# ELU chain spread over two steps for the first block only, and the attention steps, loads and weight steps around it re-timed

## The chip, the cores and the metric

The kernel runs on one core of a Trainium2 chip. The metric is the device time of one execution in microseconds (us), the median of several runs. Five queues of instructions run beside each other and wait for one another through semaphores: PE (matmuls, with their weight loads), DVE (vector work), ACT (activations, copies and casts), POOL (hardly used here) and SP, which issues nearly all DMAs. Each works through its own instructions in program order.

## What is computed

```python
# attention: chunks of 32 queries, keys from 16 before to 8 after the chunk, plus 8 memory keys
scores = scale * np.matmul(q_c, k_full.transpose(0, 1, 3, 2))
a = np.exp(scores - np.max(scores, axis=-1, keepdims=True))
a = a / (np.sum(a, axis=-1, keepdims=True) + 1e-09)
out[:, :, c_start:c_end] = np.matmul(a, v_full)
# x: (4 * 768, 8 * 64) = (3072, 512)
h = x @ w_in                                             # (3072, 2048)
g = np.where(h > 0.0, h, np.exp(np.minimum(h, 0.0)) - 1.0)
x = g @ w_out                                            # (3072, 512)
return ((x @ w1) * (x @ w2)) @ w3 @ w_out2               # (3072, 512)
```

## The kernel before

Every wide product is made of three matmuls (`mm3`, lines 124 to 126): each operand is kept as a rounded high part and the remainder, its low part, and high*high, high*low and low*high are summed in PSUM. So every operand that PE reads has to be split first: ACT writes the high part, DVE subtracts it from the value and writes the low part.

**The first two products.** The 3072 tokens are cut into 8 blocks of 384, and `w_in`, `w_out` into 16 slices each. The main loop counts n = 0 to 129, n = 16 * block + slice. In pass n PE works out `mm_h(n)`, 12 matmuls of 384 columns, one slice of h, into one of two PSUM banks (`bank4`, `bank5` in turn). ELU of that slice goes through five steps: `elu_exp` (two ACTIVATEs on ACT, lines 474 and 475), `elu_max` (DVE, line 480, the last reader of the bank), `elu_hi` (ACT, line 484) and `elu_lo` (DVE, line 488). Two passes later `mm_x(n - 2)`, again 12 matmuls, adds the slice's share to the block's result in four other banks. So `mm_h(n + 2)` needs `elu_max(n)`, and `mm_x(n)` needs `elu_lo(n)`. In the kernel before, `elu_exp(n)` and `elu_max(n)` stand in pass n, `elu_hi(n)` and `elu_lo(n)` in pass n + 1.

**Block borders.** In the first two passes of a block `mm_x(n - 2)` goes ahead of `mm_h(n)`, and after the second one `store_x1` copies the four finished banks to four tiles (ACT, DVE, ACT, DVE: lines 115 and 117) and stores them to DRAM (line 501). These tiles come from a pool of four, `f`, which the weight jobs use as well.

**Attention.** Tokens are worked on in 24 groups G of 128, three to a block. A group is a chain: `at_turn`, `at_turn2` (PE transposes, ACT copies: lines 289 to 306), `load_next` (q and k of group G + 1), `at_scores` (PE, 317), `at_max` (DVE 334, 335 and an ACT exponential, 336), `at_sum` (DVE 342 to 345), `at_norm` (DVE 354), `at_flip` (DVE 365), `at_values` (PE, 376), `at_out` (split into `xhl`, 120 and 121), `load_next_v`. Groups 0 to 2 come ahead of the loop, interleaved by hand in the string `START` (a letter for a step, a digit for the group, `f` for one step of the weight feed). The others are put into numbered slots, two to a pass: slot 2n runs in the middle of pass n and slot 2n + 1 after `mm_x(n - 2)` (in the first two passes of a block slot 2n comes after `mm_x` and slot 2n + 1 after `mm_h`). `base(G)` is the slot in which a group's chain begins; its steps follow at 0, 1, 1, 2, 3, 4, 5, 6, 8, 8 and 9.

**Weights.** `w_in` and `w_out` come as doubles and are rebuilt as float32 in 32 jobs of the feed. One `feed.step()` does a cast on ACT (172) and one Prelu (159), and on DVE a shift (163), an or (167) and a subtraction (175), spread over three jobs in a row. Five steps stand in `START`, and two in each pass of the first block until they are used up. Weights of the later products go through like jobs in the slots (`rebase`, `mid_low`, `mid_split`) of the groups from 6 on, and every `mid_low` starts a next load of 512 KB.

Of the kernel before, what the change touches and what calls it, by code (L numbers as in the profile page):

```python
# [19 lines left out]
def tile_kernel(  # L20
# [40 lines left out]
    GPB = TB // GQ  # L61
    FF1 = w_in.shape[1] // P
# [3 lines left out]

    LATER = (10, 11, 12, 13, 14, 15, 25, 26, 27, 28, 29, 30, 31)

    START = "t0 u0 f s0 t1 f m0 u1 s1 z0 n0 m1 p0 t2 v0 u2 s2 f z1 n1 p1 o0 m2 v1 f z2 n2 p2 o1 v2 f o2"
    SCALE = 1.0 / float(D) ** 0.5  # L70
    assert GQ == P and KEYS == 64 and KT == 4 and HP == 4 and DM == 512

# [177 lines left out]
    def load_qk(G):  # L250
        if G >= NG:
            return
        b, g = divmod(G, GPS)
        t0 = g * GQ - LEFT
        p0, n1 = max(0, -t0), min(LEFT + RIGHT, S - t0 - P)
        kn_g = k_t[G] = at_tile(G, qk_p, [P, 2, H, D], "kn") if 0 < G < GPB else kn
        q_t[G] = at_tile(G, qk_p, [GQ, H, D], "qn")
        eng = nc.scalar if G == 0 else nc.sync
        eng.dma_start(out=q_t[G], in_=by_token(q, b, g * GQ, (g + 1) * GQ))
        nc.sync.dma_start(out=kn_g[p0:P, 0], in_=by_token(k, b, t0 + p0, t0 + P))  # L260
        nc.sync.dma_start(out=kn_g[0:n1, 1], in_=by_token(k, b, t0 + P, t0 + P + n1))
        if g == 0 or G < GPB:
            nc.sync.dma_start(out=kn_g[LEFT + RIGHT:CH, 1], in_=by_token(mem_k, b, 0, NM))

    def load_v(G):
        if G >= NG:
            return
        b, g = divmod(G, GPS)
        t0 = g * GQ - LEFT
        p0 = max(0, -t0)  # L270
        vw_g = v_t[G] = at_tile(G, v_p, [P, 2, H, D], "vw") if 0 < G < GPB else vw
        nc.sync.dma_start(out=vw_g[p0:P, 0], in_=by_token(v, b, t0 + p0, t0 + P))
        for c in range(NCG):
            t1 = t0 + (c + 1) * CH
            n1 = min(LEFT + RIGHT, S - t1)
            nc.sync.dma_start(out=vw_g[c * CH:c * CH + n1, 1], in_=by_token(v, b, t1, t1 + n1))
            if g == 0 or G < GPB:
                nc.sync.dma_start(out=vw_g[c * CH + LEFT + RIGHT:(c + 1) * CH, 1], in_=by_token(mem_v, b, 0, NM))
# [147 lines left out]
        slots.setdefault(int(at), []).append((at, len(slots.get(int(at), ())), fn, arg))  # L426

    def base(G):
        return 2 * FF1 * (G - GPB) // GPB, "slow"

    GM = 2 * GPB
    others = [Job((raw_rows, w_out2, c, 0), store=wod[c]) for c in range(FF2)]
# [3 lines left out]
    for G in range(GPB, NG):  # L436
        s0, pace = base(G)
# [16 lines left out]
    def at_step():  # L454
        store_next()
        for _, _, fn, arg in sorted(slots.pop(slot_at[0], ()), key=lambda x: x[:2]):
            fn(arg)
        slot_at[0] += 1
# [19 lines left out]
    def elu_max(n):  # L478
        e = eg_t[n]
        nc.vector.scalar_tensor_tensor(out=e, in0=e, scalar=-1.0, in1=h_t.pop(n), op0=ALU.add, op1=ALU.max)  # L480
# [5 lines left out]
    def elu_lo(n):  # L486
        g = g_t[n]
        nc.vector.tensor_tensor(out=g[:, 1, :], in0=eg_t.pop(n), in1=g[:, 0, :].bitcast(F32), op=ALU.subtract)  # L488
# [82 lines left out]
    with tc.manual_schedule():  # L571
        def weight(i):
            if i < FF1:
                return Job((raw_cols, w_in, i), slot=i)
            return Job((raw_rows, w_out, i - FF1, 0), slot=i)

        jobs, due = [], {}
        order = sorted(range(2 * FF1), key=lambda i: i if i < FF1 else i - FF1 + 2)
        for i in order:
            due[i] = len(jobs)  # L580
            jobs.append(weight(i))
        first_late = min(due[i] for i in LATER)
        feed = Feed(jobs)

        load_qk(0)
        make_identity(nc, ident)
        nc.gpsimd.memset(kn[0:LEFT, 0], 0.0)
        nc.gpsimd.memset(vw[0:LEFT, 0], 0.0)
        for c in range(NCG):
            for s in range(2):  # L590
                nc.gpsimd.memset(odd[c * CH:(c + 1) * CH, s], float(c % 2 == s))
        feed.load(1)
        load_qk(1)
        feed.load(2)
        load_v(0)
        load_qk(2)
        load_v(1)
        feed.load(3)
        load_v(2)
        feed.load(5)  # L600
        one = dict(t=at_turn, u=at_turn2, s=at_scores, m=at_max, z=at_sum, n=at_norm, p=at_flip, v=at_values, o=at_out)
        for what in START.split():
            if what == "f":
                feed.step()
            else:
                one[what[0]](int(what[1]))
        load_qk(GPB)
        load_v(GPB)
        early_psum.close()
        psum_x = ctx.enter_context(tc.tile_pool(name="psum_x", bufs=1, space=PSUM))  # L610
        for i in range(KT):
            PS[i] = psum_x.tile([P, 512], F32, name=f"bank{i}")
        NH = NB * FF1
        for n in range(NH + 2):
            j, f, at, last = seq[n] if n < NH else (NB, n - NH, n - NH, False)
            first = at < 2 and n >= 2
            if j == NB - 1 and f == 0:
                store_next()
                mid_ctx.close()
                at_ctx.close()  # L620
                late = ctx.enter_context(tc.tile_pool(name="late", bufs=1, side="right"))
                ab_jobs = [(c, r) for c in range(FF2) for r in range(2)]
            if n == FF1:
                feed.until(len(feed.jobs) - 1)
                raw_ctx.close()
                mid_ctx = ExitStack()
                pools["raw"] = mid_ctx.enter_context(tc.tile_pool(name="raw2", bufs=2, side="right"))
                pools["st"] = mid_ctx.enter_context(tc.tile_pool(name="st_p", bufs=2, side="right"))
                mid_load(2)

            def x():
                if n >= 2:
                    if n < FF1 + 2:
                        feed.until(due[FF1 + seq[n - 2][1]])
                    mm_x(n - 2)
                    if at == 1 and n < NH:
                        store_x1(j - 1)
                if n < FF1:
                    feed.step()
                at_step()  # L640

            if first:
                x()
            if n < NH:
                if j == 0:
                    feed.until(due[f])
                mm_h(n)
            if 1 <= n <= NH:
                elu_hi(n - 1)
            if n < FF1:  # L650
                feed.step()
            if 1 <= n <= NH:
                elu_lo(n - 1)
            at_step()
            if n < NH:
                elu_exp(n)
            if not first:
                x()
            if n < NH:
                elu_max(n)  # L660
            if n >= NH - FF1:

                free = [f] if n < NH else []
                if n >= NH - FF1 + 2:
                    free.append(FF1 + n - 2 - (NH - FF1))
                for slot in free:
                    if len(s_wo) < FF2 and len(s_wo) <= len(s_w3):
                        fill(slot, wod[len(s_wo)])
                        s_wo.append(slot)
                    elif len(s_w3) < 2 * FF2:  # L670
                        half, c = divmod(len(s_w3), FF2)
                        fill(slot, w3d[half][c])
                        s_w3[half, c] = slot
                    else:
                        c, r = ab_jobs.pop(0)
                        fill(slot, wabd[c][r])
                        s_ab[c, r] = slot
            if j == NB - 1:
                if f == 4:
                    load_x1(0)  # L680
                if f == 8:
                    split_x1(0)
                    load_x1(1)
        store_x1(NB - 1)
        for half in range(2):
            for c in range(FF2):
                for i in range(KT):
                    mm_wc(half, c, i)
                    if c == FF2 - 1:
                        keep_wc(half, i)  # L690
            for i in range(KT, FF2):
                c, r = ab_jobs.pop(0)
                fill(s_w3[half, i], wabd[c][r])
                s_ab[c, r] = s_w3[half, i]
        NA = NB * FF2
        for n in range(NA + 1):
            j, f = divmod(n, FF2)
            if n < NA:
                mm_ab(n)
                if f == 2 and j + 1 < NB:  # L700
                    split_x1(j + 1)
                    if j + 2 < NB:
                        load_x1(j + 2)
            if n >= 1:
                mm_o(n - 1)
                if f == 0:
                    store_out(j - 1)
# [30 lines left out]
```

## Time and profile before

| | |
|---|---|
| median of 3 runs | 1154.38 us (1153.18 to 1154.81) |
| profiled execution | 1155.27 us, its span 1153.3 us |
| before the first `mm_h` | 0 to 39.3 us |
| block 0 (passes 0 to 15) | 39.3 to about 133 us |
| blocks 1 to 7 | about 133 to 703 us |
| the last two products | about 703 us to the end |
| PE, DVE, ACT busy share | 95%, 43%, 37% |

The page gives busy shares over the whole span, so the stages have to be looked at one by one: stretches (windows) for how full each engine is, the timeline of an engine for the start of each instruction and what ended the idle time ahead of it, the table of waits for how often the same wait comes back, and the chain of waits for what ended last.

### The profile page before, as it was taken

Reading aid. Unit: us, or ns where it says so; the run is one execution under the profiler, and the core shown is the slowest. Engines: PE = TensorE matmul, PEld = TensorE weight load, DVE = VectorE, ACT = ScalarE, POOL = GpSimd, SP = SyncE. Lnnn points to the kernel's source line nnn. Section 1 sums busy time; section 2 is a strip of 40 time slices with the busy share of each in tenths; the row PEclk is TensorE's granted clock in tenths of the full one; section 3 lists DMA queues with packets and bytes.
Section 4 is the critical chain, followed back from the end, with each engine's and each line's share of the span. In section 5 each row is a group of like instructions: output and inputs, shape, how many; then the busy total and the mean of one; then the engine's idle time right before and its main releaser. Section 6 shows DMA issues by size and latency. Waiting matters only on the chain.

```text
span 1153.3 us, 20889 instructions
## 1 busy us (share of the span) xinstructions
PE 1096.8 (95%) x8800; PEld 1029.9 (89%) x8800; DVE 493.8 (43%) x912; ACT 431.1 (37%) x897; POOL 2.1 (0%) x16
## 2 busy tenths in 40 slices
PE   4688999999999999899999999999999999999998
PEld 3588889989989899899899998799999999999997
DVE  4699655565565465555555331121222212222121
ACT  3477544454454444445444341121221212222111
POOL 0000000000000000000000000000000000000000
PEclk8699999999999999999999999999999999999999
DMA  8957344543633543544531785310000101000000
GB/s 171 288 143 205 99 150 120 158 135 109 175 110 110 173 128 109 157 129 128 155 105 40 251 286 178 109 45 28 28 28 28 55 1 56 28 28 28 1 28 28
DMA packets 153100, 124.78 MB, mean 108 GB/s; under 512 B 103856, under 2 KB 136624, under 8 KB 153008
## 3 DMA queue, kind: packets, MB, share of 16 engines
q1 hardware_dynamic: 151968, 123.20, 36.3%
q8 instruction: 69, 1.13, 0.4%
q10 hardware_dynamic: 1040, 0.26, 0.1%
q14 instruction: 23, 0.19, 0.1%
HBM read 89.88 MB, written 33.55 MB: 107 GB/s over the span
## 4 chain that ended last, share of the span: by engine, by line
PE 81%; DVE 8%; ACT 5%; DMA 3%; issue 2%; SPq 0%; DVEq 0%; ACTq 0%
PE bank L124 21%; PE bank L125 20%; PE bank L126 20%; PE banks L124 4%; PE banks L126 4%; PE banks L125 4%; DMA x1d<-st 2%; PE banks L376 2%; DVE w L175 1%; DVE g L488 1%; DVE eg L480 1%; PE banks L317 1%; DVE e L354 1%; ACT w L172 1%; PE banks L291 1%
## 5 line engine op out<-in xcount | busy, mean ns | idle before, releaser
L124 PE MATMUL bank<-xhl,w 128*128 128x384 f32 x768 | 266.4, 347 | 17.5 <-DVE eg L480 16.8
L126 PE MATMUL bank<-xhl,w 128*128 128x384 f32 x768 | 259.3, 338 | 0.0
L125 PE MATMUL bank<-xhl,w 128*128 128x384 f32 x768 | 259.2, 338 | 0.0
L124 PE MATMUL bank<-g,w 128*128 128x384 f32 x512 | 176.0, 344 | 0.0
L125 PE MATMUL bank<-g,w 128*128 128x384 f32 x512 | 172.5, 337 | 1.7 <-DVE g L488 0.8
L126 PE MATMUL bank<-g,w 128*128 128x384 f32 x512 | 171.5, 335 | 0.0
L124 PEld LDWEIGHTS bank<-xhl,w 128*128 128x128 f32 x768 | 145.6, 190 | 27.5 <-DVE eg L480 21.6
L552 DVE TENSOR_TENSOR eg<-eg,banks 128x384 f32<-128x384 f32 x64 | 35.5, 554 | 271.7 <-PE banks L126 271.7
L125 PEld LDWEIGHTS bank<-xhl,w 128*128 128x128 f32 x768 | 145.7, 190 | 3.2 <-DVE xhl L121 0.4
L126 PEld LDWEIGHTS bank<-xhl,w 128*128 128x128 f32 x768 | 145.4, 189 | 0.0
L488 DVE TENSOR_TENSOR g<-eg,g 128x384 fp32r<-128x384 f32 x128 | 71.3, 557 | 108.2 <-ACT g L484 108.2
L484 ACT CAST g<-eg 128x384 fp32r<-128x384 f32 x128 | 65.7, 513 | 127.0 <-DVE eg L480 127.0
L125 PEld LDWEIGHTS bank<-g,w 128*128 128x128 f32 x512 | 96.2, 188 | 4.8 <-DVE g L488 4.7
L124 PEld LDWEIGHTS bank<-g,w 128*128 128x128 f32 x512 | 96.1, 188 | 2.2
L126 PEld LDWEIGHTS bank<-g,w 128*128 128x128 f32 x512 | 96.1, 188 | 0.0
L551 ACT COPY eg<-bank 128x384 f32<-128x384 f32 x64 | 30.7, 480 | 170.4 <-PE bank L126 170.4
L480 DVE SCALAR_TENSOR_TENSOR eg<-eg,bank 128x384 f32<-128x384 f32 x128 | 69.9, 546 | 56.0 <-ACT eg L475 55.7
L120 ACT CAST g<-eg 128x384 fp32r<-128x384 f32 x64 | 32.8, 512 | 141.4 <-DVE eg L552 141.4
L124 PE MATMUL banks<-xhl,w 128*128 128x384 f32 x256 | 85.5, 334 | 0.0
L125 PE MATMUL banks<-xhl,w 128*128 128x384 f32 x256 | 85.5, 334 | 0.0
L126 PE MATMUL banks<-xhl,w 128*128 128x384 f32 x256 | 85.5, 334 | 0.0
L474 ACT ACTIVATE eg<-bank 128x384 f32<-128x384 f32 x128 | 62.8, 490 | 48.4 <-PE bank L126 47.8
(101 smaller groups left out, 1404.9 us busy)
## 6 DMA issues: line engine op xcount, KB each, us to landing
raw<-in_moe_w_dram SPq DMA_DIRECT2D x32, 512.0 KB
raw<-in_moe_w_out_dram SPq DMA_DIRECT2D x20, 512.0 KB
w3d<-st SPq DMA_DIRECT2D x16, 512.0 KB
wabd<-st SPq DMA_DIRECT2D x16, 512.0 KB
w<-w3d SPq DMA_DIRECT2D x16, 512.0 KB
w<-wabd SPq DMA_DIRECT2D x16, 512.0 KB
raw<-in_moe_w_in_dram SPq DMA_DIRECT2D x12, 512.0 KB
x1d<-st SPq DMA_DIRECT2D x32, 192.0 KB
```

The source lines that it names most:

```text
L120: nc.scalar.copy(hi, src)
L124: mm(o, lhsT=w_hi, rhs=x_hi, start=start, stop=False)
L125: mm(o, lhsT=w_hi, rhs=x_lo, start=False, stop=False)
L126: mm(o, lhsT=w_lo, rhs=x_hi, start=False, stop=stop)
L172: nc.scalar.copy(job.to[:, 0, :], job.f if src is None else src)
L376: mm(o, lhsT=vw[cc, u, 2 * hp + r, :], rhs=pT[cc, r, hp, u, :], start=u == 0, stop=u == 1)
L474: nc.scalar.activation(e, h_t[n], AF.Relu, scale=-1.0)
L480: nc.vector.scalar_tensor_tensor(out=e, in0=e, scalar=-1.0, in1=h_t.pop(n), op0=ALU.add, op1=ALU.max)
L484: nc.scalar.copy(g_t[n][:, 0, :], eg_t[n])
L488: nc.vector.tensor_tensor(out=g[:, 1, :], in0=eg_t.pop(n), in1=g[:, 0, :].bitcast(F32), op=ALU.subtract)
L551: nc.scalar.copy(e, pab[0])
L552: nc.vector.tensor_tensor(out=e, in0=e, in1=pab[1], op=ALU.mult)
```

## The change

Four edits. In `START` the third step of the feed moves from ahead of group 1's sum to behind group 1's values, the fourth and fifth move back too, group 2's maximum (the third group) comes ahead of group 0's output, and the loads of group 3 (the fourth group; `k` and `w`) stand right behind that output and no longer behind the whole string. `base` grows by one slot, for groups 3 to 23. And from pass 16 on all five ELU steps of a slice stand in the pass that made it: `elu_exp` ahead of the slot's work, `elu_hi` and `elu_lo` right behind `elu_max`. For passes 0 to 15 the order is the old one.

```diff
-    START = "t0 u0 f s0 t1 f m0 u1 s1 z0 n0 m1 p0 t2 v0 u2 s2 f z1 n1 p1 o0 m2 v1 f z2 n2 p2 o1 v2 f o2"
+    START = "t0 u0 f s0 t1 f m0 u1 s1 z0 n0 m1 p0 t2 v0 u2 s2 z1 n1 p1 m2 o0 k3 w3 v1 z2 n2 p2 f o1 v2 f o2 f"
...
     def base(G):
-        return 2 * FF1 * (G - GPB) // GPB, "slow"
+        return 2 * FF1 * (G - GPB) // GPB + 1, "slow"
...
-        one = dict(t=at_turn, ..., o=at_out)
+        one = dict(t=at_turn, ..., o=at_out, k=load_qk, w=load_v)
         for what in START.split():
...
-        load_qk(GPB)
-        load_v(GPB)
...
                 mm_h(n)
-            if 1 <= n <= NH:
+            spread = n < FF1
+            if 1 <= n <= FF1:
                 elu_hi(n - 1)
-            if n < FF1:
+            if spread:
                 feed.step()
-            if 1 <= n <= NH:
+            if 1 <= n <= FF1:
                 elu_lo(n - 1)
+            if n < NH and not spread:
+                elu_exp(n)
             at_step()
-            if n < NH:
+            if spread:
                 elu_exp(n)
             if not first:
                 x()
             if n < NH:
                 elu_max(n)
+            if n < NH and not spread:
+                elu_hi(n)
+                elu_lo(n)
```

DVE ahead of the main loop, from the transpose of group 0 (`pT_376`) on, before and then after; `e_372` is group 1's exponentials, `pair1_101` group 2's scores, `w0_75` the first weight slice:

```order
L365 STREAM_TRANSPOSE pT_376<-e2_368 128x1024
L163 TENSOR_SCALAR f_315<-f_315 128x512
L167 SCALAR_TENSOR_TENSOR f_315<-raw_197,f_315 128x512
L175 TENSOR_TENSOR w0_75<-f_259,w0_75 128x512
L342 TENSOR_REDUCE sm_469<-e_372 128x8
L343 TENSOR_SCALAR sm_469<-sm_469 128x8
L344 RECIPROCAL sm_469<-sm_469 128x8
L345 TENSOR_TENSOR rc_470<-sm_469,odd_167 128x16
L354 TENSOR_TENSOR e2_475<-e_372,rc_470 128x16x32 x2
L365 STREAM_TRANSPOSE pT_478<-e2_475 128x1024
L121 TENSOR_TENSOR xhl0_73<-banks_94,xhl0_73 128x2x4x64
L334 TENSOR_REDUCE mx_482<-pair1_101 128x8
```

```order
L365 STREAM_TRANSPOSE pT_376<-e2_368 128x1024
L342 TENSOR_REDUCE sm_461<-e_372 128x8
L343 TENSOR_SCALAR sm_461<-sm_461 128x8
L344 RECIPROCAL sm_461<-sm_461 128x8
L345 TENSOR_TENSOR rc_462<-sm_461,odd_167 128x16
L354 TENSOR_TENSOR e2_467<-e_372,rc_462 128x16x32 x2
L365 STREAM_TRANSPOSE pT_470<-e2_467 128x1024
L334 TENSOR_REDUCE mx_472<-pair1_101 128x8
L335 TENSOR_TENSOR e_473<-pair1_101,mx_472 128x512
L121 TENSOR_TENSOR xhl0_73<-banks_94,xhl0_73 128x2x4x64
```

The three weight instructions are gone from between group 0's transpose and group 1's sum, and group 2's maximum and subtraction stand ahead of group 0's low part (L121).

SP at the end of `START`, before and then after; `more_`, `raw_` are weight loads, `qn`, `kn_166`, `vw_165` group 3's q, k and v:

```order
L140 DMA raw_317<-in_moe_w_in_dram 128x4x256
L148 DMA raw_467<-in_moe_w_out_dram 128x1024
L140 DMA raw_525<-in_moe_w_in_dram 128x4x256
L148 DMA raw_578<-in_moe_w_out_dram 128x1024
L259 DMA qn_582<-in_q_dram 128x8x64
L260 DMA kn_166<-in_k_dram 128x8x64
L261 DMA kn_166<-in_k_dram 24x8x64
L272 DMA vw_165<-in_v_dram 128x8x64
L276 DMA vw_165<-in_v_dram 24x8x64 x4
```

```order
L140 DMA raw_317<-in_moe_w_in_dram 128x4x256
L259 DMA qn_479<-in_q_dram 128x8x64
L260 DMA kn_166<-in_k_dram 128x8x64
L261 DMA kn_166<-in_k_dram 24x8x64
L272 DMA vw_165<-in_v_dram 128x8x64
L276 DMA vw_165<-in_v_dram 24x8x64 x4
L148 DMA raw_537<-in_moe_w_out_dram 128x1024
L140 DMA raw_579<-in_moe_w_in_dram 128x4x256
L148 DMA raw_589<-in_moe_w_out_dram 128x1024
```

Group 3's loads pass three weight loads.

DVE at the border of blocks 1 and 2, from the two copies of `store_x1` (`bank1`, `bank3`) on, before and then after; `eg` and `g` with `bank4`, `bank5` are the ELU tiles, `st` with `f` is the low part of a later weight:

```order
L163 TENSOR_SCALAR f_1665<-f_1665 128x512
L167 SCALAR_TENSOR_TENSOR f_1665<-raw_1636,f_1665 128x512
L480 SCALAR_TENSOR_TENSOR eg_1696<-eg_1696,bank4_95 128x384
L117 COPY st_1715<-bank1_596 128x384
L117 COPY st_1721<-bank3_598 128x384
L326 MEMSET banks_94 32x2x4x16
L175 TENSOR_TENSOR st_1757<-f_1665,st_1757 128x512
L488 TENSOR_TENSOR g_1772<-eg_1696,g_1772 128x384
L334 TENSOR_REDUCE mx_1776<-banks_94 128x8
L335 TENSOR_TENSOR e_1777<-banks_94,mx_1776 128x512
L480 SCALAR_TENSOR_TENSOR eg_1781<-eg_1781,bank5_96 128x384
L488 TENSOR_TENSOR g_1797<-eg_1781,g_1797 128x384
```

```order
L480 SCALAR_TENSOR_TENSOR eg_1667<-eg_1667,bank4_95 128x384
L488 TENSOR_TENSOR g_1686<-eg_1667,g_1686 128x384
L117 COPY st_1704<-bank1_596 128x384
L117 COPY st_1710<-bank3_598 128x384
L163 TENSOR_SCALAR f_1683<-f_1683 128x512
L167 SCALAR_TENSOR_TENSOR f_1683<-raw_1636,f_1683 128x512
L326 MEMSET banks_94 32x2x4x16
L175 TENSOR_TENSOR st_1775<-f_1683,st_1775 128x512
L480 SCALAR_TENSOR_TENSOR eg_1739<-eg_1739,bank5_96 128x384
L488 TENSOR_TENSOR g_1779<-eg_1739,g_1779 128x384
L334 TENSOR_REDUCE mx_1798<-banks_94 128x8
L335 TENSOR_TENSOR e_1799<-banks_94,mx_1798 128x512
```

The weight job's shift and or (L163, L167) move behind the two copies, the low part of the block's first slice (first L488) ahead of them, and the next slice's maximum and low part (second L480 and L488) ahead of the group's maximum (L334, L335).

## Rows read from the trace of the kernel before

**Rows 1.** The page, busy us (share of the span) xinstructions of each engine

```profile
PE 1096.8 (95%) x8800; PEld 1029.9 (89%) x8800; DVE 493.8 (43%) x912; ACT 431.1 (37%) x897; POOL 2.1 (0%) x16
```

**Rows 2.** Stretches: from:to, length, busy of each engine, granted PE clock, DMA share, GB/s

```profile
30.00:40.00 10.00, 3.80 (x97) 3.02 (x89) 8.83 (x17) 4.68 (x9) 0.00 (x0) 0.50 1.00 350
40.00:50.00 10.00, 6.29 (x24) 5.26 (x25) 2.62 (x5) 2.66 (x7) 0.00 (x0) 0.67 1.13 257
39.30:130.00 90.70, 76.53 (x757) 71.07 (x757) 76.58 (x143) 58.13 (x120) 0.00 (x0) 0.93 0.64 169
```

**Rows 3.** Timeline of DVE ahead of the loop: start, us, instruction [idle before <-releaser]

```profile
19.79 1.23 DVE L365 STREAM_TRANSPOSE pT<-e 128x1024 f32<-128x1024 f32 x1
24.06 0.69 DVE L175 TENSOR_TENSOR w<-f,w 128x512 fp32r<-128x512 f32 x1 [2.00 <-ACT w L172]
24.67 0.68 DVE L342 TENSOR_REDUCE sm<-e 128x8 f32<-128x512 f32 x1
27.36 1.25 DVE L365 STREAM_TRANSPOSE pT<-e 128x1024 f32<-128x1024 f32 x1
...
35.10 1.25 DVE L365 STREAM_TRANSPOSE pT<-e 128x1024 f32<-128x1024 f32 x1
...
39.28 0.69 DVE L121 TENSOR_TENSOR xhl<-pair,xhl 128x512 fp32r<-128x512 f32 x1 [0.70 <-ACT xhl L120]
```

**Rows 4.** Timeline of SP and DVE around the start of block 0

```profile
27.73 0.36 SPq L148 DMA_DIRECT2D raw<-in_moe_w_out_dram  x1
38.46 0.39 SPq L259 DMA_DIRECT2D qn<-in_q_dram  x1
...
50.51 0.69 DVE L175 TENSOR_TENSOR w<-f,w 128x512 fp32r<-128x512 f32 x1 [7.82 <-ACT w L172]
53.38 0.55 DVE L488 TENSOR_TENSOR g<-eg,g 128x384 fp32r<-128x384 f32 x1
```

**Rows 5.** Chain of waits, two of its DMAs: start, us to landing, what

```profile
38.95 7.50 DMA kn<-in_k_dram
...
225.93 4.16 DMA x1d<-st
```

**Rows 6.** Who waited for whom, whole span: us in total, times, longest

```profile
DVE st L117 <- DMA x1d<-st: 23.1, 6, 4.4
PE bank L124 <- DVE eg L480: 16.8, 15, 1.8
```

**Rows 7.** Timeline of PE at the second block border, first matmul of each piece

```profile
223.83 0.45 PE L124 MATMUL bank<-g,w 128*128 128x384 f32 x1
226.54 0.86 PE L317 MATMUL banks<-kT,qT 64*32 64x64 f32 x64
231.60 0.34 PE L124 MATMUL bank<-g,w 128*128 128x384 f32 x1
235.46 0.44 PE L124 MATMUL bank<-xhl,w 128*128 128x384 f32 x1 [1.36 <-DVE eg L480]
237.68 0.33 PE L124 MATMUL bank<-g,w 128*128 128x384 f32 x1
240.71 0.44 PE L124 MATMUL bank<-xhl,w 128*128 128x384 f32 x1 [0.79 <-DVE eg L480]
```

**Rows 8.** Timeline of SP and DVE at the same border

```profile
225.49 0.35 SPq L148 DMA_DIRECT2D raw<-in_moe_w_out_dram  x1
230.21 0.56 DVE L117 COPY st<-bank 128x384 f32<-128x384 f32 x1 [3.85 <-DMA x1d<-st]
234.85 0.56 DVE L480 SCALAR_TENSOR_TENSOR eg<-eg,bank 128x384 f32<-128x384 f32 x1 [1.69 <-ACT eg L475]
239.04 0.42 DVE L163 TENSOR_SCALAR f<-f 128x512 int32<-128x512 int32 x1
239.50 0.69 DVE L167 SCALAR_TENSOR_TENSOR f<-raw,f 128x512 int32<-128x512 int32 x1
```

**Rows 9.** Stretch in which the border's fourth store moves, columns as in rows 2

```profile
231.40:232.00 0.60, 0.60 (x5) 0.33 (x4) 0.60 (x2) 0.00 (x0) 0.00 (x0) 1.00 0.64 230
```

More of the change, by code (lines that the diff above doesn't have):

```diff
@@ L600, in tile_kernel @@
         feed.load(5)
-        one = dict(t=at_turn, u=at_turn2, s=at_scores, m=at_max, z=at_sum, n=at_norm, p=at_flip, v=at_values, o=at_out)
+        one = dict(t=at_turn, u=at_turn2, s=at_scores, m=at_max, z=at_sum, n=at_norm, p=at_flip, v=at_values, o=at_out, k=load_qk, w=load_v)
         for what in START.split():
```

## The prediction, made before the changed kernel ran

> **What bounds the kernel now.** I read the page first: PE is busy for 95% of the span, DVE and ACT for well under half [rows 1]. That says that in most of the program only PE's own instructions count, so an edit to DVE, ACT or SP can pay only where PE stands still. I therefore went through PE's timeline piece by piece, a piece being the 12 matmuls of one `mm_h` or `mm_x`. Undisturbed, a piece takes 2.08 us (for instance 235.46 to 237.68 is one, with 0.1 us more because attention work stood before it) [rows 7]. The reader is to see in that timeline which pieces are longer. Inside blocks 1 to 7 hardly any is. There are two places where PE loses time.
>
> The first is everything up to the end of block 0. The stretch 39.3 to 130 has DVE busy for 76.6 of 90.7 us [rows 2], and the largest hole in DVE is one wait of 7.82 us for a cast on ACT [rows 4]. Without it DVE is busy for 76.6 of 83 us: two weight steps a pass, ELU and attention are nearly more than DVE can do in the 4.2 us that PE needs for a pass. Block 0 is bound by DVE, and what DVE gains at its start, the block's end gains.
>
> The second is each block border that has attention in it. `mm_x` of the old block's last slice takes 2.71 us (223.83 to 226.54) where 2.19 would do; the first `mm_x` of the new block is followed by `mm_h` 3.86 us later (231.60 to 235.46), and the next one 3.03 us later (237.68 to 240.71), where 2.08 would do [rows 7]. That is 0.5 + 1.8 + 0.95 = 3.25 us a border. The table of waits says what PE waited for in the last two, `elu_max`, the reader of its bank (16.8 us in all), and it shows the cause behind it: DVE's second copy in `store_x1` waits for a store to land, 6 times, 23.1 us in all [rows 6]. Six borders, so some 19.5 us.
>
> **The start (START string).** Removed from ahead of group 1's sum: a weight step on DVE, whose subtraction waited 2.00 us for ACT. Group 0's transpose is at 19.79 and takes 1.23, so the sum can start at 21.0 instead of 24.67 [rows 3]. From sum to transpose is 2.69 us (24.67 to 27.36) [rows 3], so group 1's transpose moves to 23.7. Then come group 2's maximum and subtraction and group 0's low part on DVE, about 0.7 each as the rows of that size have it [rows 3], and two ACT operations of about 0.6 in between: group 2's sum at 28.2, its transpose at 30.9 instead of 35.10 [rows 3]. The weight steps are not gone, they now stand behind it: two steps of 0.42 + 0.69 + 0.69 [rows 4, 8], the low part of group 1 and that of group 2 follow the 1.25 us transpose. So group 2's low part, which the second matmul of `mm_h(0)` needs, starts at about 36.2 instead of 39.28 [rows 3]: 3 us earlier. The fifth weight step now comes behind it, 1.8 us more work on DVE inside block 0, which the reckoning at the next step includes.
>
> **Group 3's loads.** Before, they were issued at 38.46, behind a weight load that waited for DVE, and k landed at 38.95 + 7.50 = 46.45 [rows 4, 5]. Now only six weight loads of 512 KB stand ahead, the first issued at 27.73 [rows 4]. At 350 GB/s [rows 2] they take 9.0 us and are through at about 37.7; 512 KB of q and k at 257 GB/s [rows 2] take 2.0 us more. That gives 39.7 as the earliest; I add some 2 us because the 16 engines do not finish together, and take 42, with 46.5 (nothing gained) as the other end. Three weight loads come later by these 0.8 MB, about 3 us; the DMA share in block 0 is 0.64 [rows 2], so they have slack.
>
> What follows: before, from k's landing to the first `elu_lo` (53.38) it was 6.9 us [rows 4, 5], because `elu_exp(0)`, a weight cast and subtraction and `elu_max(0)` all stood behind group 3's transposes and copies on ACT. With the chain one slot later they stand ahead and are done while k is on its way. Left behind the landing are the transposes and copies (2.6 us), `elu_hi`, a cast, a subtraction: about 4.5 us. So the first `elu_lo` comes at 42 + 4.5 = 46.5 instead of 53.38. I take **6.5 us** for the start as a whole, and as its ends 2.4 (landing at 46.5) and 8. From there the same instructions remain for DVE, so block 0 ends earlier by as much. PE's clock was granted at 0.50 and 0.67 in these stretches [rows 2], that is at 1.2 GHz for part of them; since DVE sets the pace I count nothing for it.
>
> **Base one slot later, ELU in one pass: the borders.** Three things change at a border. (a) `elu_hi` and `elu_lo` of the old block's last slice no longer stand behind group copies on ACT, so the 0.5 us go. (b) The weight job's `mid_low`, which starts a 512 KB load, now comes behind `store_x1`. Before, that load was issued 0.44 us ahead of the stores (225.49) [rows 8], and the first store took 4.16 us [rows 5]. The fourth store, with nothing ahead of it, is copied from 230.21 to 230.77 [rows 8] and has moved 138 of its 192 KB (128 x 384 float32) by 232.0 [rows 9]: about 1.6 us. I take 1.6 for the first store too, the row of the same transfer, with 4.16 as the other end. (c) On DVE, from the waiting copy to the end of `elu_max` it was 5.2 us (230.21 to 235.41) [rows 8], with a low part, the group's maximum and subtraction and an exponential in it; now there are a shift and an or (0.42, 0.69) [rows 8], one cast and one subtraction of about 0.65, and `elu_max`: 3.4 us.
>
> Against this, ACT has the three group copies, a Prelu and `elu_hi` ahead of the first copy, so that the store is issued some 1.3 us later, seen from the next `mm_x`. Set out from that `mm_x`'s start: before, the copy waited until -1.4 and `elu_max` ended at +3.8, 1.8 us too late for +2.08. Now the copy ends its wait at -1.4 + 1.3 - 2.5 = -2.6 and `elu_max` ends at +0.8: no wait. The step after it (the 0.95) has the group's sum ahead of `elu_max` as before, with under 1 us of room by the same reckoning; I leave 0.35 us a border for it. So 2.9 us a border, **17.4 us** for six. With a landing of 4.16 again, `elu_max` ends at +3.3 and the later wait stays too: 1.1 us a border, 6.6 in all. The upper end is 3.25, 19.5 in all.
>
> The Trainium skill, page "DMA: Bandwidth & Descriptors", section "Anatomy of one DMA", puts a DMA at about 2.0 us fixed plus its bytes at 436 GB/s, fitted there on another issue path: 2.45 us for 192 KB, an estimate from that page. The 1.6 us of the fourth store is shorter than that. By that page of the skill the copy would wait 0.85 us longer, the later step would lose about 0.6 us a border, and the sum would be 3.6 us smaller, near 1134.
>
> The same page of the Trainium skill, section "Queues, rings and completion order", says that descriptors on one engine are consumed in ring order. The 4.16 against 1.6 us agrees; for group 3's early loads it speaks against the change, since the weights behind them wait.
>
> **Inside the blocks** the edit costs nothing by my reckoning. The five ELU steps are 0.5 to 0.56 each [rows 4, 8], 1.6 us from the end of `mm_h(n)` to that of `elu_max(n)`, and `mm_h(n + 2)` starts three pieces later, 6.24 us: 4.6 us are left for slot work on DVE and ACT. What hides it is that distance; the rivals price its loss.
>
> **Sum.** 1155.27 for the profiled execution, less 6.5, less 17.4, is 1131.4. The median of the runs is 0.9 below that execution: **1130.5 us**.
>
> **Rivals.** (1) *The stores still land late*, because store, v loads and weight traffic from the last slots are still in the engines. For it: the DMA share of 0.64 in block 0 shows how much is moved at times [rows 2]. Against it: the next load now stands behind. 6.5 + 6.6 gained: about 1141.5. (2) *The start gives little*: six weight loads ahead and the ragged end of the 16 engines [rows 2] let k land no earlier, or the weight steps moved out of the start's holes come back on DVE, which is nearly full. 1.5 + 17.4: about 1135.5. (3) *Slower: ACT and DVE wait for each other in each pass.* `elu_hi(n)` now waits on ACT for `elu_max(n)`, which stands behind the slot's DVE work, and `elu_exp(n + 1)` queues behind `elu_hi(n)`. In the slot with `at_values` and `at_out`, `elu_max` waits for a piece of PE (2.08), the values (about 1.2), a cast and a subtraction (about 1.3): 4.6 us, just the room that there is. From there on PE stops. If the 18 groups of blocks 1 to 6 lose 2 us each, the size of the waits of that kind now (1.8) [rows 6], that is 36 us: 1131 + 36 = 1167. Against it: in that slot the values themselves also push `mm_h(n + 2)` back by their own length. (4) *The waits only change their name*: PE stops later in the border for the next `elu_max`, and the start is given back by DVE: about 1154.
>
> **Chances.** Forecast 0.60, (1) 0.12, (2) 0.16, (3) 0.07, (4) 0.05. The forecast's own range is 1125 to 1135. Cases (1) and (2) have the same sign, so the range reaches over both, to 1143, and down to 1121, which takes both upper ends and something for waits inside block 0 that I did not count. About 0.2% is what a measurement of this kernel can tell from no change. Faster 0.88, within it 0.05, slower 0.07.
>
> **What would show it.** In the profile of the changed kernel: the first `elu_lo` near 46.5 and k's landing near 42; block 0 over some 6 us earlier; no wait of DVE's copy for a store above 2 us; the waits of `mm_h` for `elu_max` down from 15 to the few of block 0; the distance between borders about 80 us instead of 83. It would be wrong if the granted clock or the last two products changed, or if ACT's `elu_hi` were followed by PE waits inside the blocks.

## The result and the profile after

| | before | after |
|---|---|---|
| median of the runs, us | 1154.6 | 1127.88 |
| lowest to highest, us | 1153.18 to 1155.08 | 1127.37 to 1129.28 |
| ratio after / before | | 0.9773, interval 0.9756 to 0.9789 |
| span of the profiled execution, us | 1153.3 | 1127.3 |
| `elu_max(13)` starts (end of block 0) | 127.98 | 122.58 |
| from there to `elu_max(125)` (blocks 1 to 7) | 561.81 | 541.24 |

The kernel became 2.3% faster: 26.7 us between the medians, 26.0 us between the two spans. The last two rows of the table say where: 5.4 us before `elu_max(13)`, 20.6 us between it and `elu_max(125)`, and nothing in the two last products. These two distances, read from the starts of `elu_max` on DVE, are what every experiment below is measured by.

The page after, first row of busy times (answers to [rows 1]), and stretches of the kernel after (columns as in [rows 2]: length, busy of PE, PEld, DVE, ACT, POOL, granted clock, DMA share, GB/s):

```profile
PE 1092.1 (97%) x8800; PEld 1029.9 (91%) x8800; DVE 493.7 (44%) x912; ACT 430.2 (38%) x897; POOL 2.1 (0%) x16
...
30.00:40.00 10.00, 5.90 (x74) 5.31 (x75) 9.83 (x17) 4.17 (x7) 0.00 (x0) 1.00 1.06 334
40.00:50.00 10.00, 8.74 (x99) 7.40 (x99) 6.41 (x13) 7.37 (x16) 0.00 (x0) 1.00 0.87 258
...
127.80:677.00 549.20, 549.12 (x5311) 529.24 (x5309) 297.94 (x553) 267.50 (x566) 0.00 (x0) 1.00 0.52 152
```

The same stretch of blocks 1 to 7 in the kernel before:

```profile
133.06:703.06 570.00, 555.21 (x5309) 529.77 (x5309) 297.45 (x552) 268.48 (x565) 0.00 (x0) 1.00 0.49 146
```

The same 5309 or so matmuls: before, PE stood still for 14.8 us and was 6.1 us longer at its work; after, it is busy for 549.12 of 549.20 us. Hardly any wait of PE is left there.

The start of the kernel after: `lo` of group 2, the transposes of group 3, the second ELU step of the first slice, and from the chain of waits the load of group 3 (answers to [rows 3], [rows 4] and [rows 5]):

```profile
36.27 0.68 DVE L121 TENSOR_TENSOR xhl<-pair,xhl 128x512 fp32r<-128x512 f32 x1
41.66 1.12 PE L289 MATMUL banks<-ident,qn 128*128 128x128 f32 x4 [0.76 <-DMA qn<-in_q_dram]
42.76 1.11 PE L291 MATMUL banks<-ident,kn 128*128 128x128 f32 x4
46.85 0.55 DVE L488 TENSOR_TENSOR g<-eg,g 128x384 fp32r<-128x384 f32 x1
...
31.43 10.19 DMA qn<-in_q_dram
```

Group 2's low part starts at 36.27 (39.28 before), the loads of group 3 are issued 7 us earlier and k is used from 42.76 (46.50 before), the first `elu_lo` starts at 46.85 (53.38 before).

The second border after: PE's pieces, then SP and DVE (answers to [rows 7] and [rows 8]), then the two waits of [rows 6] in the whole span:

```profile
214.45 0.42 PE L124 MATMUL bank<-g,w 128*128 128x384 f32 x1
217.08 0.44 PE L124 MATMUL bank<-xhl,w 128*128 128x384 f32 x1
...
222.36 0.33 PE L124 MATMUL bank<-g,w 128*128 128x384 f32 x1
224.44 0.33 PE L124 MATMUL bank<-xhl,w 128*128 128x384 f32 x1
226.52 0.33 PE L124 MATMUL bank<-g,w 128*128 128x384 f32 x1
228.60 0.33 PE L124 MATMUL bank<-xhl,w 128*128 128x384 f32 x1
```

```profile
217.52 2.91 SPq L501 DMA_DIRECT2D x1d<-st  x4
220.53 1.58 SPq L259 DMA_DIRECT2D qn<-in_q_dram  x1
...
217.62 0.55 DVE L117 COPY st<-bank 128x384 f32<-128x384 f32 x1
219.53 0.56 DVE L117 COPY st<-bank 128x384 f32<-128x384 f32 x1 [1.35 <-PE bank L126]
222.44 0.55 DVE L480 SCALAR_TENSOR_TENSOR eg<-eg,bank 128x384 f32<-128x384 f32 x1
227.41 0.55 DVE L480 SCALAR_TENSOR_TENSOR eg<-eg,bank 128x384 f32<-128x384 f32 x1
```

```profile
DVE st L117 <- PE bank L126: 10.0, 7, 2.4
DVE st L117 <- DMA x1d<-st: 3.2, 2, 1.7
PE bank L124 <- DVE eg L480: 3.5, 3, 1.5
```

From 222.36 on the pieces follow each other every 2.08 us, where 3.86 and 3.03 stood before [rows 7]. The second copy on DVE still waits, 1.35 us instead of 3.85 [rows 8]. The row names PE, but the last matmul into that bank was over by 216.72, when PE's next step starts. What the copy waits for is the first store's landing, that is, the moment when its tile is free again: 219.53 - 217.52 = 2.0 us after the store's issue, where it was 4.28 (230.21 less 225.93) [rows 5, 8]. PE's waits for `elu_max` are down from 15 to 3, all of them in block 0.

### The profile page after: what moved, and what is told of

The parts are those of the page before. It is cut to its first block, busy times and chain, and to the rows that moved or that the text cites. A ratio compares the mean times of both kernels' runs of the same rounds, so it can differ in the third digit from the quotient of the medians.

```text
span 1127.3 us, 20869 instructions
## 1 busy us (share of the span) xinstructions
PE 1092.1 (97%) x8800; PEld 1029.9 (91%) x8800; DVE 493.7 (44%) x912; ACT 430.2 (38%) x897; POOL 2.1 (0%) x16
## 4 chain that ended last, share of the span: by engine, by line
PE 89%; DVE 3%; ACT 3%; DMA 2%; SPq 1%; issue 1%; ACTq 0%
PE bank L124 24%; PE bank L126 23%; PE bank L125 23%; PE banks L124 4%; PE banks L126 4%; PE banks L125 4%; PE banks L376 2%; PE banks L317 1%; DMA vw<-in_v_dram 1%; ACT w L172 1%; DVE w L175 1%; PE banks L289 1%; DMA qn<-in_q_dram 1%; PE banks L291 1%; PE banks L407 1%; PE banks L303 1%
## 5 line engine op out<-in xcount | busy, mean ns | idle before, releaser
L484 ACT CAST g<-eg 128x384 fp32r<-128x384 f32 x128 | 65.8, 514 | 161.5 <-DVE eg L480 161.5
L488 DVE TENSOR_TENSOR g<-eg,g 128x384 fp32r<-128x384 f32 x128 | 71.4, 557 | 88.3 <-ACT g L484 86.7
L480 DVE SCALAR_TENSOR_TENSOR eg<-eg,bank 128x384 f32<-128x384 f32 x128 | 69.6, 544 | 52.8 <-ACT eg L475 52.8
```

Source lines behind the costliest of these rows:

```text
L484: nc.scalar.copy(g_t[n][:, 0, :], eg_t[n])
```

## The experiments

The median is of a kernel's own runs, the ratio is to runs of before on the same chip, and the last two columns come from its trace. There is no kernel 9. "Block 0" is the start of `elu_max(13)`; "blocks 1 to 7" runs from there to `elu_max(125)`.

| kernel | median, us | ratio to before, interval | block 0 | blocks 1 to 7 |
|---|---|---|---|---|
| before | 1154.6 | | 127.98 | 561.81 |
| after | 1127.88 | 0.9773 (0.9756 to 0.9789) | 122.58 | 541.24 |
| 1 ELU edit alone | 1140.68 | 0.9891 (0.9876 to 0.9907) | 126.03 | 551.25 |
| 2 `base` alone | 1134.46 | 0.9833 (0.9818 to 0.9849) | 124.86 | 544.34 |
| 3 start alone | 1149.92 | 0.9967 (0.9955 to 0.9978) | 122.86 | 561.94 |
| 4 ELU and `base` | 1131.47 | 0.9803 (0.9787 to 0.9820) | 125.03 | 541.80 |
| 5 after, group 3 loaded late | 1132.70 | 0.9825 (0.9810 to 0.9839) | 126.86 | 541.05 |
| 6 before, no fourth copy | 1133.02 | 0.9829 (0.9813 to 0.9846) | 126.19 | 541.10 |
| 7 after, a copy ahead of the stores | 1128.91 | 0.9795 (0.9780 to 0.9809) | 120.96 | 542.40 |
| 8 after, no shift in the feed | 1126.07 | 0.9766 (0.9746 to 0.9787) | 120.55 | 541.53 |
| 10 before, load behind the stores | 1139.83 | 0.9885 (0.9867 to 0.9902) | 125.68 | 546.97 |
| 11 after, two more stores ahead | 1134.42 | 0.9842 (0.9826 to 0.9858) | 121.05 | 548.24 |
| 12 after, fourth group later | 1126.64 | 0.9774 (0.9755 to 0.9793) | 120.01 | 541.38 |

One thing has to be read first, the scatter of the start. Kernels 1, 6 and 10 are the kernel before up to the first border, and their traces have 126.03, 126.19 and 125.68 where the trace of before has 127.98. Kernels 7 and 11 are the kernel after up to there: 120.96 and 121.05 against 122.58. The means are 126.5 (four traces) and 121.5 (three). A difference under 2 us in the column "block 0" says nothing. The granted clock does not explain it: in the stretches 30 to 40 and 40 to 50 it was 1.00 and 0.96 (near 2.4 GHz) in kernel 1, but 0.50 (1.2 GHz) and 0.67 in kernels 6 and 10, and the three end block 0 within 0.5 us of each other.

**1, 2 and 4: the two edits at the border, alone and together.** The edit of 1 is the diff's part on ELU, that of 2 one line, and 4 has both:

```diff
-        return 2 * FF1 * (G - GPB) // GPB, "slow"
+        return 2 * FF1 * (G - GPB) // GPB + 1, "slow"
```

> The kernel before with only the ELU edit (all five steps in one pass from pass 16 on); START and base as before. The weight load still goes out ahead of the first store, so that store should land in about 4.2 us as before. Theory 'landing' (base alone mends the borders, by letting the stores go first): at most 1 us a border, 6 us in all, about 1148, and PE's waits for elu_max stay near 15. Theory 'order' (what counts is what stands on DVE between the late copy and elu_max, now 5.2 us): the low part and the exponential ahead of elu_max are gone, about 3 us a border, 18 us in all, about 1136. Theory 'either' (each of the two edits gives more room than the 1.8 us that are missing): also about 1136, and base alone gives as much. The start and block 0 stay as they were.

> The kernel before with only base one slot later; ELU and START as before. 'Landing' and 'either': the weight load goes behind the stores, the copy waits some 2 us instead of 4, elu_max ends before PE wants the bank: 18 us at the borders. 'Order': the group's work is a slot later too, but the low part of the slice before still stands between, so little, 1150. In block 0 group 3's transposes go behind elu_exp(0) though k lands as late as before: 2.4 us (the lower end that the prediction gave). So 1134 by the first two, 1150 by the last.

> ELU and base edits together, START and the loads of group 3 as before. The six borders as in the changed kernel (20.7 us there) and 2.4 us at the start: about 1131.5. If the two edits add up, this is 1154.6 less the gains of the two single ones; by 'either' it is only 2 to 5 us below the better of them.

Who waited for whom in the whole span, kernel 1 and then kernel 2:

```profile
DVE st L117 <- DMA x1d<-st: 22.4, 6, 4.3
PE bank L124 <- DVE eg L480: 11.1, 13, 2.0
```

```profile
DVE st L117 <- DMA x1d<-st: 8.1, 6, 1.4
PE bank L124 <- DVE eg L480: 1.5, 1, 1.5
```

With ELU alone DVE's copy waits as long as before (22.4 us against 23.1), since the 512 KB load still stands ahead of the stores; blocks 1 to 7 gain 10.6 us all the same, because less stands between that copy and `elu_max`. With `base` alone the copy's wait falls to 8.1 us, PE's wait for `elu_max` goes, and 17.5 us are gained. Together they give 20.0, not 28.0: both fill the same hole. That is theory 'either' for kernels 2 and 4 (1134 was expected and 1134.46 measured; 4 is 3.0 below 2). Kernel 1, at 1140.68, lies between the 1136 of 'either' and 'order' and the 1148 of 'landing': the order on DVE alone gives half, `base` alone nearly all. Since `base` moves work of the group on DVE as well as the load, kernel 2 does not say which of them counts; kernel 10 below does. Neither edit is idle, and a gain that is split by edits is not a sum of their single gains.

**6: the wait taken away.** The tile for the fourth bank is not taken and not copied in blocks 0 to 6; the third is stored in its place, so part of the result is left out.

```diff
-            t = f_p.tile([P, 512], F32, tag="f", name="st")
-            copy_on("av"[o % 2], t[:, 0:TB], PS[o][:, 0:TB])
+            if o < KT - 1 or j == NB - 1:
+                t = f_p.tile([P, 512], F32, tag="f", name="st")
+                copy_on("av"[o % 2], t[:, 0:TB], PS[o][:, 0:TB])
```

> The kernel before; in blocks 0 to 6 the fourth bank of store_x1 is not copied and the third tile is stored in its place, so the copy that waits for the first store's landing is left out (and part of the block's result with it). If that wait is what starts the chain behind it, elu_max comes some 4 us earlier at each border, and PE's waits of 1.8 and 0.95 us go: 16 us, about 1138; the 0.5 us ahead of the last mm_x stay. If the wait is not the cause (ACT's order, or the group's work on DVE), 3 us at most, from the copies themselves.

Blocks 1 to 7 take 541.10 us, as in the kernel after (541.24), with no other edit: 20.7 us gained, more than the 16 expected. The copy itself, 0.56 us on DVE, goes with its wait, but that is 3.4 us in six borders; the copy that waits for a tile is what PE lost its time to. A fifth tile in the pool, which would take away the wait and leave nothing out, was not tried.

**10: only the order on SP.** The load of `mid_low` is held back at a border until the four stores have been issued; PE, DVE and ACT keep their order.

```diff
-        mid_load(mid_jobs.index(job) + 3)
+        behind.append(mid_jobs.index(job) + 3)
+        if not hold[0]:
+            mid_load(behind.pop())
...
                         store_x1(j - 1)
+                        hold[0] = False
+                        while behind:
+                            mid_load(behind.pop())
```

> The kernel before, with one edit: at the six borders the load that mid_low starts (512 KB) is issued behind the four stores of store_x1 instead of ahead of them. Nothing moves on PE, DVE or ACT. Theory 'landing': the first store lands in about 2 us instead of 4.16, the wait of DVE's copy falls from 3.85 to about 1.5 us a border, elu_max ends 2.3 us earlier and the first of the two PE waits (1.8 us a border) goes, the second (0.95) shrinks: 10 to 17 us, so 1137 to 1144. Theory 'order': the store's landing hardly counts, the gain of the borders is from what DVE does behind the copy: 1150 to 1154, with the copy's wait still above 3 us.

SP and DVE at the second border, the next wait of PE there, and the sum of these waits:

```profile
219.36 2.91 SPq L504 DMA_DIRECT2D x1d<-st  x4
222.32 0.66 SPq L148 DMA_DIRECT2D raw<-in_moe_w_out_dram  x1
...
221.36 0.56 DVE L117 COPY st<-bank 128x384 f32<-128x384 f32 x1 [1.31 <-ACT g L487]
231.86 0.45 PE L124 MATMUL bank<-xhl,w 128*128 128x384 f32 x1 [0.16 <-DVE eg L483]
...
PE bank L124 <- DVE eg L483: 6.9, 11, 1.8
```

The store's tile comes free 2.0 us after its issue (219.36 to 221.36) instead of 4.28, the copy waits 1.31 us instead of 3.85, the first PE wait of the border is gone and the second is 0.16 instead of 0.79 [rows 7]. Blocks 1 to 7 gain 14.8 us from this alone, 72% of what the change gains there. Theory 'landing' holds. In the kernel after, the next group's q and k loads stand behind the stores too (220.53); the landing does not need that, for in kernel 10 they still went out ahead, the last at 217.59.

**11: the landing made late again in the kernel after.**

```diff
+            if o == 0 and j < NB - 2:
+                for i in range(2):
+                    nc.sync.dma_start(out=spare[:, i, :], in_=t[:, 0:TB])
             nc.sync.dma_start(out=x1d[j][:, o, :], in_=t[:, 0:TB])
```

> The changed kernel, with one edit: at the six borders the first finished tile is stored twice more, to a place that nobody reads, ahead of its real store, so that 384 KB stand in the rings ahead of that store and its tile comes free later. The DMA waits for the same copy as the store, so it cannot run ahead of time. Theory 'landing': the fourth copy waits some 2 us longer (about 3.4 instead of 1.35 at the second border), elu_max ends 2 us later, PE gets waits for it again at each border of 0.6 to 1.8 us: 1132 to 1139. Theory 'order': with the short chain behind the copy there is room enough, no new PE wait: 1127 to 1130.

The same places:

```profile
217.18 0.82 SPq L504 DMA_DIRECT2D spare<-st  x2
218.06 3.19 SPq L505 DMA_DIRECT2D x1d<-st  x4
...
220.34 0.56 DVE L118 COPY st<-bank 128x384 f32<-128x384 f32 x1 [2.51 <-DMA x1d<-st]
228.83 0.44 PE L125 MATMUL bank<-xhl,w 128*128 128x384 f32 x1 [0.41 <-DVE eg L481]
```

The tile is free 3.16 us after the first of the extra stores was issued (217.18 to 220.34), where it was 2.0 us after the first issue in the kernel after: 1.15 us later. PE waits again, at the later of the border's two steps, and blocks 1 to 7 take 7.0 us more, 1.2 a border. In the kernel after, `elu_max` of that step ends at 227.96 (227.41 + 0.55) and PE's next step begins at 228.60. So the change leaves 0.64 us of room there: a little more traffic ahead of the stores costs again.

**7, a miss.** The same was tried first with a copy of 512 KB from DRAM to DRAM, issued ahead of the stores:

```diff
+            nc.sync.dma_start(out=spare, in_=w_out2.bitcast(I32)[0:P, 0:1024])
             for o in range(KT):
```

> The changed kernel with one copy of 512 KB from DRAM to DRAM, read by nobody, issued on SP right ahead of the four stores of each of the first six borders. The first store should land about 2 us later, near 4.2 us as before the change. By the landing's share: the copy waits 2 us longer, elu_max ends 0.6 us after PE wants the bank, the one behind it about 0.8: some 1.5 us a border, 9 us in all, about 1137. If the order on DVE alone carries the gain, within 1 us of the changed kernel.

```profile
211.15 0.51 SPq L500 DMA_DIRECT2D spare<-in_moe_w_out_dram  x1
215.96 2.97 SPq L504 DMA_DIRECT2D x1d<-st  x4
```

The copy waits for nothing, so SP issued it 4.8 us ahead of the stores and it was out of their way: the store's tile was free at 218.02, 2.06 us after the issue, as in the kernel after. Its time is the one expected if the order on DVE alone carried the gain, but with no late landing in it the run says nothing on that; in kernel 11 the extra transfer reads the tile that is stored, and so cannot run ahead.

**3 and 5: the start.** 3 has the new `START` (with the moved loads) alone; 5 is the kernel after with group 3's loads behind the whole string, as before:

```diff
-    START = "... m2 o0 k3 w3 v1 z2 n2 p2 f o1 v2 f o2 f"
+    START = "... m2 o0 v1 z2 n2 p2 f o1 v2 f o2 f"
...
+        load_qk(GPB)
+        load_v(GPB)
```

> The kernel before with only the new START string and group 3's early loads; base and ELU as before. Borders unchanged. k lands near 42 as in the changed kernel; group 3's transposes still stand ahead of elu_exp(0) on ACT, 6.9 us from landing to the first elu_lo, so that comes at about 49 instead of 53.4: 4.5 us, about 1150. The rival (the start gives little) expects 1153 or more.

> The changed kernel with group 3's q, k and v loaded behind the whole START string, as before the change. The rest of START is new. k should land near 46 again, about 4 us later than in the changed kernel, and PE's wait for it opens again at the start. Theory 'loads' (the early loads carry most of the gain at the start): 3 to 4 us slower than the changed kernel, about 1131.5. Rival 'DVE' (DVE's earlier weight steps and the later transposes carry it, since DVE has other work while k is on its way): within 1 us of it, 1128 to 1129.

Kernel 5 at the start, PE waiting for group 3's q, and the first `elu_lo`:

```profile
36.96 0.69 PE L125 MATMUL bank<-xhl,w 128*128 128x384 f32 x1 [0.91 <-DVE xhl L121]
45.22 1.12 PE L289 MATMUL banks<-ident,qn 128*128 128x128 f32 x4 [4.47 <-DMA qn<-in_q_dram]
50.37 0.55 DVE L488 TENSOR_TENSOR g<-eg,g 128x384 fp32r<-128x384 f32 x1
```

With late loads group 2's low part is as early as in the kernel after, but PE waits 4.47 us for q, and block 0 ends at 126.86, no earlier than before (126.5). So all of the start's gain hangs on the early loads: theory 'loads' holds. The start alone ends block 0 at 122.86 (3.6 less than 126.5; 4.5 had been expected), `base` alone at 124.9 (1.6 less, inside the scatter); both together 121.5 (5.0 less).

**8: is block 0 bound by DVE?** The feed's shift is left out of the kernel after, so that `w_in` and `w_out` are not fully rebuilt and each weight step has one 0.42 us instruction less on DVE.

```diff
-            self.do(i - 1, shift, low)
+            self.do(i - 1, low)
```

> The changed kernel without the shift (L163) in the feed's 32 weight jobs, so that the first two weights are wrong: 0.46 us less on DVE for each of some 29 steps in block 0, 13 us. If DVE sets block 0's pace, block 0 gets shorter until PE's own work binds: 6 to 9 us, 1119 to 1122. If the hand-overs between ACT and DVE or the loads set it: under 2 us, 1126 or more.

Block 0 from 45 to 125, the kernel after and then kernel 8:

```profile
45.00:125.00 80.00, 70.00 (x679) 65.95 (x678) 70.57 (x133) 54.41 (x112) 0.00 (x0) 0.98 0.63 182
```

```profile
45.00:125.00 80.00, 70.14 (x702) 65.78 (x704) 62.30 (x110) 53.77 (x111) 0.00 (x0) 0.97 0.63 182
```

DVE has 8.3 us less to do in this stretch, and block 0 ends at 120.55 instead of 121.5, inside the scatter. So the amount of DVE's work does not bind block 0. PE is busy for 70 of the 80 us in both, and in the kernel after the rest is some 10 us of waits for attention steps and `elu_max`. That PE's work and these hand-overs set the pace is read from this and was not tested by itself.

**12: the fourth group's chain another slot later.**

```diff
-        return 2 * FF1 * (G - GPB) // GPB + 1, "slow"
+        return 2 * FF1 * (G - GPB) // GPB + (2 if G == GPB else 1), "slow"
```

> The changed kernel, with one edit: the chain of the fourth group alone begins another slot later, so that mm_h(1) stands ahead of its transposes and the wait for k is covered by it. If what holds up the start of block 0 is k's landing (PE stands from 37.7 to 41.7 us in the changed kernel), mm_h(1) fills 2.1 us of that and the start gains 1 to 2 us: 1125.5 to 1127. If it is the weights and the low part of group 2 that mm_h(0) and mm_h(1) need, nothing moves, or the chain ends later and costs: 1127 to 1130.

```profile
43.21 0.60 PE L289 MATMUL banks<-ident,qn 128*128 128x128 f32 x4
43.65 0.60 PE L291 MATMUL banks<-ident,kn 128*128 128x128 f32 x4
46.81 0.43 PE L303 MATMUL banks<-ident,kn 32*128 32x32 f32 x4 [2.56 <-ACT kT L297]
```

The transposes of group 3 no longer wait for a load, but PE waits 2.56 us for ACT one step further on. The median, 1126.64, lies in the range expected for a gain, but the ratio to before on its own chip is that of the kernel after (0.9774 and 0.9773), and block 0 ends at 120.01 instead of 121.5, inside the scatter: no gain is shown.

## Why the prediction was right

The forecast was 1130.5 with a range of 1121 to 1143; the median is 1127.88. The sum was 6.5 + 17.4 = 23.9; the traces have 5.4 + 20.6 = 26.0. The first term was too large and the second too small, so the total came nearer than the second term did, which is luck.

**The borders, 17.4 against 20.6.** The mechanism is as forecast, step by step. (b) The landing was taken as 1.6 and measured 2.0 us (217.52 to 219.53). The 1.6 was read from bytes moved [rows 9]; in the kernel after, the stretch from 217.52 to 219.00 moved 133 GB/s, which is just the bytes of one store, and the tile was free 0.5 us after that. (c) From the waiting copy to the end of `elu_max` 3.4 was forecast; it is 219.53 to 222.99, 3.46. Seen from the next `mm_x` (222.36), the copy's wait ends at -2.8 (forecast -2.6) and `elu_max` ends at +0.6 (forecast +0.8), before the +2.08 at which PE wants its bank. That these fit so closely is partly luck: the landing was shortened by 2.27 us and not by 2.56, but the stores were issued only 0.8 us later, seen from that `mm_x`, where 1.3 was forecast. The step behind has 0.64 us of room (under 1 was forecast). (a) The 2.71 us piece is gone: 214.45 to the next step at 216.72 is 2.27. What was off is the size: 0.35 us a border were set aside for the later wait, and that wait went as well; and the upper end, 3.25 us a border, came from three pieces of one border, while the whole stretch had 14.8 us of standing still and 6.1 us of longer matmul time to give, 3.5 a border. The 14.8 could be read before the change, in the row of the stretch of blocks 1 to 7 shown above; the 6.1 shows only beside the row after. One reading of the prediction was wrong without harm: 235.46 to 237.68 [rows 7] is 2.22 us and follows a wait for `elu_max`, not attention work; an undisturbed piece is 222.36 to 224.44 above.

**The price of a landing.** Counted from the store's own issue, the tile came free after 4.28 us behind a 512 KB load, 2.28 us behind two stores of its own size (218.06 to 220.34 in kernel 11), and 2.0 with nothing ahead. With the estimate of 2.45 us from the Trainium skill, page "DMA: Bandwidth & Descriptors", section "Anatomy of one DMA", the forecast would have been near 1134; the 2.0 us measured lie between that and the 1.6 taken. The same page of the Trainium skill, section "Queues, rings and completion order", says that each DMA engine takes descriptors in the order of the ring; the three landings agree.

**The start, 6.5 against 5.4 (5.0 between the means of the traces).** Group 2's low part came at 36.27 (forecast 36.2), k was used from 42.76 (its landing forecast at 42) and the first `elu_lo` at 46.85 (46.5). The term is still too large, and two reasons are seen. Its zero was one execution in which group 3's landing was late: PE's first use of k is at 46.50 in the trace of before and at 45.0 to 45.1 in kernels 1, 6 and 10, whose start is the same. And the first `elu_lo` is not the mark by which block 0 is passed on: group 3's scores now stand ahead of that pass's work, and they came 5.8 us earlier (53.62 to 47.84), not 6.5. The sum for the landing has a slip: 27.73 + 9.0 is 36.7, not 37.7, so its earliest end was 38.7. The margin covered it: q landed at 41.62 (31.43 + 10.19), and PE went on to k right behind it.

**The reading "block 0 is bound by DVE" was wrong.** [rows 2] have PE busy for 76.53 and DVE for 76.58 of the 90.7 us; the prediction read one of two equal columns. Kernel 8 decides against it. The sum survived since the gain at the start reached the block's end all the same.

**The rivals.** (1) Late stores: the condition did not arise. Its price was 1.8 us a border for a tile 2.56 us later; kernel 11, with the tile 1.15 us later, costs 1.2. (2) A small gain at the start: k landed as forecast. (3) ACT does wait more for `elu_max` (161.5 us in 107 waits, 127.0 in 99 before), but PE has 0.08 us of idle time in blocks 1 to 7: nothing reached it. (4) No new wait took the place of the old one. The distance between borders is 79.5 to 79.8 us at the second to fifth border, where about 80 was named. One sign of being wrong did appear: the mean granted clock of the profiled executions rose from 0.986 to 0.998. It did not make the gain, since the runs of before on one chip with a clock of 0.985 to 0.988 took 1151.7 to 1154.4 us, and those with 0.997 to 0.999 took 1152.4 to 1154.0.

## What to carry to other kernels

A buffer pool that is one tile short shows as an engine's copy waiting for a store, and the store's landing is set by what was issued ahead of it on the same queue: put the stores of a border ahead of the next big load before anything is reordered on the engines. Take the upper end of such a gain from PE's idle time over the whole stage and from its longer pieces at all borders, not from the pieces of one. An engine's busy share only says that it binds when no other column of the same row is as high, and a start that hangs on a DMA landing should be read from more than one execution.

## What was not expected of the hardware

SP's own issue of a load can take long. The two k loads of group 3 in the kernel after, in a stretch with a DMA share of 1.06:

```profile
32.09 4.24 SPq L260 DMA_DIRECT2D kn<-in_k_dram  x1
36.43 3.97 SPq L261 DMA_DIRECT2D kn<-in_k_dram  x1
```

At the border of kernel 10 the larger of the two was issued in 0.53 us for a later group. Busy DMA engines alone do not explain it: the 512 KB weight load and the q load issued just ahead, at 30.84 and 31.43, took 0.49 and 0.56 us. An early load can thus also hold up SP, here for 8 us; why it is the k loads was not tried.

In the stretches 30 to 40 and 40 to 50 the granted clock was 1.00 (2.4 GHz) in the trace of the kernel after and 0.50 (1.2 GHz) and 0.67 in that of kernel 5. Yet the matmul at 36.96 or 37.01 took 0.69 us in both, and those behind it 0.52 us each, one every 0.32 us, where block 1 has 0.33, one every 0.17. The record of the clock alone does not explain these; what does stays open.
